# The last two column chunks of a split float32 sequence product as one Strassen step: sums of one operand's tiles made in DRAM, those of the other by VectorE

## The chip, the cores and the metric

One NeuronCore of a Trainium2 chip runs the whole kernel. TensorE multiplies, VectorE, ScalarE and GpSimd (POOL) work on tiles in SBUF, and transfers are issued by SyncE (the SP queue), by ScalarE's queue and, after the change, by POOL's. The metric is the device time of one launch in microseconds (us); a profiled execution gives the span from the first to the last instruction beside it.

## What is computed

```python
a = einsum("bsd,ed->bse", x, dft_hid_re);  b = einsum("bsd,ed->bse", x, dft_hid_im)
y = einsum("ts,bse->bte", dft_seq_re, a) - einsum("ts,bse->bte", dft_seq_im, b)
# peer(x): q = x w_q; scores of 32 heads x 2 halves against 16 keys each; the best 2 of each half,
# the best 2 of the 4 sums, softmax g; act = gelu(x . u[expert]); out = sum g * act * v[expert]
g = sigmoid((x * gate_w).sum(-1))
return g * y + (1 - g) * peer(x)
```

x is 2048 x 640 and both sequence matrices are 2048 x 2048, all float32. Each row of x picks experts out of 256.

## The kernel before

Every large product is made from float32 operands cut in two: `split` lets ScalarE copy the high part (L122) and POOL or VectorE subtract it for the low part (L123). `mm3` then issues three matmuls per tile product, high x high, high x low, low x high (L127 to L129). The sequence product is made first: with C the cosine or sine matrix, C x is computed transposed, in 128 steps n, one per 128 x 512 piece of C. A piece is (w, c, s): w is cosine or sine, c one of four chunks of 512 columns, s one of 16 row tiles. A step has 5 column tiles of x and so 15 matmuls, adding up in 5 PSUM banks over 16 steps; then 5 results of 128 x 512 are copied to the stage tile ST, multiplied by the gate (L192) and stored to DRAM as pd, by w and c. The 16 row tiles of x stay in SBUF in split form (X0 to X15).

The emission order is written by hand. `at(n, f)` puts f behind step n, and engines execute what they are given in order. A piece is loaded five steps ahead by SP (`wf`, L159) and split three steps ahead on POOL into a ring of four (`WS`). Steps 0 to 30 carry the preparation of the query weights beside them; steps 31 (N0) to 63 the scores (15 more matmuls a step), with their selection on VectorE and, every fourth block, the gates (L456 to L486); N1 is 64. From step 64 on the matrices of the hidden product are loaded and split (`load_dd`, `split_dd`, `draw`, `DD`).

Behind that runs `experts`, a background generator that a credit pump (`bg`) advances between groups of matmuls: 32 tiles, each with three VectorE operations that build one-hot tables (`build`, L580 to L582, tile `hot`, four sets), 16 small matmuls on TensorE (`use`, L603) and two VectorE operations that gather the result (`sums`, L589 and L591). Tiles go in pairs: while a pair is being built, the pair before is used. Near the end of the sequence product a `drain` forces out what is left of a tile so that a buffer can change its use.

The hidden product follows as one Strassen–Winograd step (seven half-size products, `UNITS`) for each half of the rows, 70 steps of 9 or 6 matmuls, pieces split five steps ahead into a ring of six. Its sums on the DFT side come from `make_sums` (five VectorE operations, L688 to L692) and `split_sums`, at steps NPC-14 to NPC-5; those on the pd side from `load_parts`, `sum_parts` (L770 to L774) and `store_parts`, at steps 96 to 111, into DRAM tiles pq. NPC is 128 here.

Of the kernel before, what the change touches and what calls it, by code (L numbers as in the profile page):

```python
# [16 lines left out]
P = 128  # L17
# [11 lines left out]
NPC = 2 * NC * NT  # L29
# [6 lines left out]
PAIR = 2 * TC  # L36
NSTEP = 7 * KD
# [53 lines left out]
def gated_mix_kernel(ctx: ExitStack, tc: tile.TileContext, xT, xn, dreT, dimT, wsre, wsim, wq, kT, uT, vv, gw, out):  # L91
# [40 lines left out]
    pq = {u: dram.tile([KD, P, TC], F32, name=f"pq{u}", tag=f"pq{u}") for u in ("s1", "s2", "s4", "s3")}  # L132
# [15 lines left out]
    gt = const.tile([P, NT], F32)  # L148

# [31 lines left out]
    grow, staged, P22 = {}, {}, {}  # L181
# [14 lines left out]
    def store_piece(q):  # L196
        w, c = divmod(q, NC)
        if q == NC + 1:
            P22.update((d, staged[q, d]) for d in range(KD))
        for d in range(KD):  # L200
            nc.scalar.dma_start(pd[w, c][d], staged.pop((q, d)))
# [21 lines left out]
    for q in range(2 * NC):  # L223
# [341 lines left out]
    def experts():  # L565
# [18 lines left out]
        def sums(g, c, t):  # L584
            if c == 0:
                store_gates(g - 1)
                cd[g] = p3.tile([P, E, P], F32, name="cd", tag="cd")
            tmp = p3.tile([P, 8 * E, 4], F32, name="tmp")
            nc.vector.tensor_tensor(tmp, t.rearrange("p m (e t) -> p (m e) t", t=4),  # L589
                                    mask4[:, None, :].to_broadcast([P, 8 * E, 4]), op=OP.mult)  # L590
            nc.vector.tensor_reduce(cd[g][:, :, 8 * c:8 * c + 8].rearrange("p e m -> p m e"),  # L591
                                    tmp.rearrange("p (m e) t -> p m e t", e=E), op=OP.add, axis=AX.X)
            if c == 15:
                summed[g] = cd[g]

        def use(group):
            ts = []
            for g, c, s in group:
                t = bank(7, (P, 8, E * 4)) if last_part else ps_s((P, 8, E * 4))
                pt, qt = (HOT[s // 2][:, s % 2, n].rearrange("p (m c) -> p m c", m=16) for n in range(2))  # L600
                for m in range(16):
                    r = slice(64 * (m % 2), 64 * (m % 2) + 64)
                    nc.tensor.matmul(t[r, m // 2, :], pt[:, m], qt[:, m], start=True, stop=True)  # L603
                ts.append(t)
                free_sets.append(s)
            for (g, c, s), t in zip(group, ts):
                sums(g, c, t)
                yield 1.4
# [24 lines left out]
    def load_dd(m):  # L633

        if m < KD:
            draw[m] = big.tile([P, 2, D], F32, name="draw", tag=("xf", "xh", "xl")[m % 3])
# [13 lines left out]
    for m in range(3):  # L650
        at(N1 + m, load_dd, m)
    for m in range(KD):
        for a in range(2):
            at(N1 + 3 + 2 * m + a, split_dd, m, a)
        at(N1 + 4 + 2 * m, load_dd, m + 3)
# [13 lines left out]
    def load_dt(k):  # L669
        T[k] = big.tile([P, 2, D], F32, name="dt", tag=("xf", "xh")[k % 2])  # L670
        for w in range(2):
            nc.sync.dma_start(T[k][:, w], (dreT, dimT)[w][k])
# [9 lines left out]
    def make_sums(k):  # L682
        if k == 0:
            T["t"] = big.tile([P, 9 * P], F32, name="tf", tag="xl")
        f, t = T.pop(k), T["t"]
# [7 lines left out]
        bg.credit -= 3.0  # L693

    def split_sums(k):
        for n in [k] + ([5 + k // 2] if k % 2 == 0 else []):
            TS[n] = big.tile([P, 2 * D], F32R, name="ts", tag=f"X{(1, 3, 4, 5, 6, 0, 2, 7)[n]}")
# [6 lines left out]
    def load_v():  # L704
        T["f"] = big.tile([P, 2, D], F32, name="dt", tag="xf")
        nc.sync.dma_start(T["f"], vv.rearrange("k p d -> p k d"))

    def split_v():

        for t in ("xh", "xl"):  # L710
            T[t] = big.tile([P, 2, D], F32R, name="v" + t, tag=t)
        split(T["f"], T["xh"], T["xl"], nc.vector)
# [6 lines left out]
    for k in range(KD):  # L719
        at(NPC - 17 + 2 * k, load_dt, k)  # L720
        at(NPC - 14 + 2 * k, make_sums, k)
        at(NPC - 13 + 2 * k, split_sums, k)
    at(NPC - 3, load_v)
    at(NPC, split_v)
    at(NPC + 28, store_gates, 1)


    raw_free, raw_tags = deque(), [("wf", 1)] * 5 + [(f"X{s}", 2) for s in range(10, 16)] + [("xf", 2)]
    raw, sp = {}, {}

    def take(key):
        if raw_tags:
            t, n = raw_tags.pop(0)
            if t == "wf":
                raw_free.append(big.tile([P, TC], F32, name="ra", tag=t, bufs=5))
            else:
                r = big.tile([P, 2, TC], F32, name="ra", tag=t)
                raw_free.extend(r[:, a] for a in range(2))
# [6 lines left out]
    def load_a(b, what, k, row, col):  # L745
        f = take((b, what, k))
        nc.sync.dma_start(f, pd[col - 1, 2 * b + row - 1][k] if row else pq[what][k])
# [7 lines left out]

    PS, parts = [], {}

    def load_parts(k):

        if not PS:  # L760
            PS.extend(big.tile([P, 2, TC], F32, name="ps", tag=t) for t in ("xf", "xh", "xl"))
        parts[k] = [t[:, k % 2] for t in PS]
        for f, q in zip(parts[k], ((0, 1), (0, 0), (1, 0))):
            nc.sync.dma_start(f, pd[q][k])

    def sum_parts(k, n):
        f21, f11, f12 = parts[k]
        f22 = P22[k]
        if n == 0:
            nc.vector.tensor_add(f22, f22, f21)  # L770
            nc.vector.tensor_add(f21, f21, f11)
        else:
            nc.vector.tensor_add(f11, f11, f22)
            nc.vector.tensor_add(f12, f12, f11)  # L774
        bg.credit -= 1.5

    def store_parts(k, n):
        f21, f11, f12 = parts[k]
        for u, f in (("s2", f11), ("s4", f12)) if n else (("s1", P22[k]), ("s3", f21)):
            nc.sync.dma_start(pq[u][k], f)  # L780

    for k, (n, m) in enumerate(((-1, 2), (0, 4), (5, 7), (7, 9), (10, 12))):
        n, m = NT * (NC + 2) + n, NT * (NC + 2) + m
        at(n, load_parts, k)
        for a in range(2):
            at(m + a, sum_parts, k, a)
            at(m + 2 + a, store_parts, k, a)

# [3 lines left out]
    def split_step(m):  # L792
        if m < 2 * NSTEP:
            b, (u, k) = m // NSTEP, divmod(m % NSTEP, KD)
            what = UNITS[u]
            key = (b, "s" if b and what in ("s1", "s2", "s4") else what, k)
            sp[m] = ring(m)[:, 0], ring(m)[:, 1]
            split(raw[key], *sp[m], nc.vector if what in ("s2", "s3") else nc.gpsimd)
            bg.credit -= 0.8 if what in ("s2", "s3") else 0.0
            if b == 0 or what in ("a11", "a12", "a22", "s3", "s4"):  # L800
                give(key)
# [17 lines left out]
    def split_z(b, n):  # L819

        if not zop:
            for k in range(2):
                zop[k] = big.tile([P, 2, TC], F32R, name="zo", tag=f"X{8 + k}")
# [68 lines left out]
    def step(m):  # L892
# [13 lines left out]
        split_step(m + AHEAD)  # L906
# [8 lines left out]
        h, l = sp.pop(m)  # L915
# [23 lines left out]
        if what == "s3":  # L939
            at(NPC + m, post, b, what)  # L940
            at(NPC + m, quarter, b)
        elif not very_last:
            at(NPC + m + 1, post, b, what)
# [11 lines left out]
    def quarter(b):  # L955
        roles["Y"] = [bank(3), bank(4)]
        z_group("Y", 2, None, first=True, last=True)
        at(NPC + b * NSTEP + 6 * KD, post, b, "q")

    M = NPC  # L960
    for k in range(KD):
        at(M - 6 + k, load_a, 0, "a11", k, 1, 1)
        at(M - 4 + min(k, 3), load_a, 0, "a12", k, 1, 2)
        at(M + k // 2, load_a, 0, "s1", k, 0, 0)
        at(M + 2 + k, load_a, 0, "s2", k, 0, 0)
        at(M + 7 + k, load_a, 0, "s4", k, 0, 0)
        at(M + 12 + k, load_a, 0, "s3", k, 0, 0)
        at(M + 18 + k, load_a, 0, "a22", k, 2, 2)
    M = NPC + NSTEP
# [12 lines left out]
    for b in range(2):  # L982
        M = NPC + b * NSTEP
        for n, i in ((0, -1), (1, 21)):
# [25 lines left out]
    last_part = True  # L1010
    for m in range(2 * NSTEP):
        share = 0.95 if m >= 5 else 0.0
        step(m)
        follow(NPC + m)
# [46 lines left out]
```

## Time and profile before

| | |
|---|---|
| device time, 3 runs | 788.47 to 789.88 us, median 788.64 |
| device time of the profiled execution | 788.32 us |
| its span | 786.4 us |
| TensorE busy | 774.7 us (99%), 4116 matmul instructions, mean granted clock 0.996 |
| VectorE, ScalarE, POOL busy | 547.8 us (70%), 275.5 us (35%), 335.9 us (43%) |
| DMA | 130.31 MB, 166 GB/s over the span |

The span is 1.92 us shorter than the device time of the same execution. A busy TensorE counts overlapping matmuls, so the mean duration of one is longer than the distance between two starts; the distance is what a matmul costs. The score steps end near 394 us, the last gates near 421 us, step 85 starts at 465.7 us, and the hidden product starts near 624 us.

### The profile page before, as it was taken

To read this page: it belongs to the slowest core of one execution; us is meant where nothing else is said; L and a number is where in the kernel's file an instruction comes from. 1 tells how busy PE (TensorE), PEld (TensorE's weight loads), DVE (VectorE), ACT (ScalarE), POOL (GpSimd) and SP (SyncE) were. 2 spreads that over 40 slices of the span, in tenths; PEclk is the share of its full clock that TensorE was granted. 3 is DMA by queue.
4 is the path that set the end of the run, shared out by engine and by line. 5 is a ranking of instruction groups with operands and counts; after the bars stand their busy time and mean duration, and the time that the engine had idled before them with its cause. 6 is when DMAs were issued, how large, how long until landed. Compare 5 with 4: busy or idle time off the path is not lost.

```text
span 786.4 us, 11008 instructions
## 1 busy us (share of the span) xinstructions
PE 774.7 (99%) x4116; PEld 624.5 (79%) x4116; DVE 547.8 (70%) x660; ACT 275.5 (35%) x445; POOL 335.9 (43%) x233
## 2 busy tenths in 40 slices
PE   9999999999999999999999999999999899999997
PEld 6777677887888888878888888888888688888886
DVE  6741122287898899999894178799799948836651
ACT  5334323321224524523533711311324353334350
POOL 5423224314414323244159643344456483468270
PEclk9999999999999999999999999999999899999999
DMA  9966995402213142130355342568744695459321
GB/s 347 373 243 189 324 337 187 165 13 88 64 38 99 49 154 83 51 124 29 97 188 171 119 146 85 158 227 277 255 172 162 212 322 185 132 174 320 121 81 67
DMA packets 75508, 130.31 MB, mean 166 GB/s; under 512 B 17088, under 2 KB 24128, under 8 KB 75200
## 3 DMA queue, kind: packets, MB, share of 16 engines
q1 hardware_dynamic: 62704, 112.18, 42.6%
q10 hardware_dynamic: 12752, 17.45, 6.1%
q8 instruction: 32, 0.52, 0.3%
q14 instruction: 20, 0.16, 0.1%
HBM read 102.84 MB, written 25.17 MB: 163 GB/s over the span
## 4 chain that ended last, share of the span: by engine, by line
PE 88%; issue 8%; POOL 2%; DVE 1%; ACT 0%; DMA 0%; ACTq 0%; SPq 0%; DVEq 0%; POOLq 0%
PE b L127 28%; PE b L129 28%; PE b L128 27%; PE b L320 2%; POOL xl L123 2%; PE b L603 1%; PE b L332 1%; PE b L213 0%; DMA wf<-in_wsre 0%; DVE tf L690 0%; DVE tmp L589 0%; ACT L390 0%; ACT WS L122 0%; DVE tf L691 0%; DVE tf L692 0%
## 5 line engine op out<-in xcount | busy, mean ns | idle before, releaser
L123 POOL TENSOR_TENSOR WS<-wf,WS 128x512 fp32r<-128x512 f32 x127 | 190.8, 1508 | 284.8 <-ACT WS L122 284.7
L127 PE MATMUL b<-WS,X 128*128 128x512 f32 x635 | 252.3, 397 | 0.1
L128 PE MATMUL b<-WS,X 128*128 128x512 f32 x635 | 248.6, 391 | 0.0
L129 PE MATMUL b<-WS,X 128*128 128x512 f32 x635 | 248.5, 391 | 0.0
L127 PEld LDWEIGHTS b<-WS,X 128*128 128x128 f32 x635 | 119.9, 189 | 33.1 <-issue 7.8
L129 PEld LDWEIGHTS b<-WS,X 128*128 128x128 f32 x635 | 119.7, 189 | 25.4
L128 PEld LDWEIGHTS b<-WS,X 128*128 128x128 f32 x635 | 120.0, 189 | 23.8 <-POOL WS L123 0.3
L122 ACT ACTIVATE WS<-wf 128x512 fp32r<-128x512 f32 x128 | 79.8, 627 | 145.8 <-PE b L129 66.2
L129 PE MATMUL b<-WU,xl 128*128 128x512 f32 x160 | 63.2, 395 | 2.2 <-POOL xl L123 1.7
L123 POOL TENSOR_TENSOR xl<-xf,xh 128x640 fp32r<-128x640 f32 x16 | 32.1, 2031 | 71.0 <-ACT xh L122 71.0
L127 PE MATMUL b<-WU,xh 128*128 128x512 f32 x160 | 62.4, 390 | 0.0
L128 PE MATMUL b<-WU,xh 128*128 128x512 f32 x160 | 62.3, 390 | 0.0
L423 ACT ACTIVATE sc<-b 128x512 f32<-128x512 f32 x32 | 20.1, 629 | 112.5 <-PE b L129 112.5
L123 POOL TENSOR_TENSOR WS<-ra,WS 128x512 fp32r<-128x512 f32 x32 | 46.0, 1459 | 29.9 <-ACT WS L122 29.2
L437 DVE TENSOR_REDUCE mm<-sc 128x64 f32<-128x1024 f32 x32 | 38.9, 1216 | 26.5 <-ACT sc L423 26.0
L192 DVE SCALAR_TENSOR_TENSOR ST<-ST,grow 128x512 f32<-128x512 f32 x40 | 34.6, 930 | 31.8 <-DMA grow<-gdr 31.8
L335 DVE TENSOR_TENSOR WU<-b,WU 128x512 fp32r<-128x512 f32 (+1 forms) x16 | 7.9, 491 | 56.6 <-ACT WU L334 56.6
L439 DVE TENSOR_TENSOR eq<-sc,mm 128x1024 f16<-128x1024 f32 x32 | 43.4, 1355 | 1.1
L123 POOL TENSOR_TENSOR WP<-ra,WP 128x512 fp32r<-128x512 f32 x18 | 27.7, 1550 | 32.9 <-ACT WP L122 32.7
L443 DVE TENSOR_REDUCE rr<-eq 128x64 f16<-128x1024 f16 x32 | 39.0, 1220 | 1.1
L589 DVE TENSOR_TENSOR tmp<-b,mask 128x512 f32<-128x512 f32 x32 | 22.0, 688 | 25.4 <-PE b L603 24.5
L129 PEld LDWEIGHTS b<-WU,xl 128*128 128x128 f32 x160 | 30.1, 188 | 11.2 <-POOL xl L123 5.1
(148 smaller groups left out, 1244.7 us busy)
## 6 DMA issues: line engine op xcount, KB each, us to landing
wq<-in_wq SPq DMA_DIRECT2D x32, 640.0 KB, 6.7
wf<-in_wsre SPq DMA_DIRECT2D x64, 256.0 KB, 5.2
wf<-in_wsim SPq DMA_DIRECT2D x64, 256.0 KB, 3.6
ra<-pd SPq DMA_DIRECT2D x50, 256.0 KB, 3.4
pd<-ST ACTq DMA_DIRECT2D x40, 256.0 KB, 3.6
xr<-in_xn SPq DMA_DIRECT2D x16, 320.0 KB, 5.8
xf<-in_xT SPq DMA_DIRECT2D x16, 320.0 KB, 3.3
ra<-pqs SPq DMA_DIRECT2D x20, 256.0 KB, 4.3
```

The lines of the kernel that those rows point to most:

```text
L122: nc.scalar.activation(h, f, AF.Copy)
L123: eng.tensor_sub(l, f, h.bitcast(F32))
L127: nc.tensor.matmul(o, wh, ah, start=first, stop=False, skip_group_check=more)
L128: nc.tensor.matmul(o, wh, al, start=False, stop=False, skip_group_check=more)
L129: nc.tensor.matmul(o, wl, ah, start=False, stop=last, skip_group_check=more)
L192: nc.vector.scalar_tensor_tensor(f, f, -1.0 if w else 1.0, g, op0=OP.mult, op1=OP.mult)
L320: nc.tensor.matmul(ps[32 * j:32 * j + 32, :HALF], kp[:, 8 * G // H, r, :], w[:, j], start=(r == 0), stop=(r == 1))
L423: nc.scalar.activation(scs[i].rearrange("p h e -> p (h e)")[:, c], ps, AF.Copy)
L437: nc.vector.tensor_reduce(m, sc, op=OP.max, axis=AX.X)
L439: nc.vector.tensor_tensor(eq, sc, m[:, :, None].to_broadcast([P, HH, E]), op=OP.is_equal)
L443: nc.vector.tensor_reduce(r, eq, op=OP.max, axis=AX.X)
L589: nc.vector.tensor_tensor(tmp, t.rearrange("p m (e t) -> p (m e) t", t=4), mask4[:, None, :].to_broadcast([P, 8 * E, 4]), op=OP.mult)
```

## The change

NPC is now 96: six of the eight chunks are made as before. The last two (sine, columns 1024 to 2047) become one Strassen–Winograd step over a 2 x 2 grid of blocks of C (each 8 row tiles by 512 columns) and of x, in 56 steps G (QS) of 9 matmuls (a11, a12, s1, a22) or 6 (s2, s4, s3): 432 matmuls in place of 480. The hidden product starts at step LP = 152.

- Sums of C's tiles (`cq`, 4 x 8 tiles of 128 x 512) and of pd's (`pq`, 4 x 5 tiles) are made in DRAM: `copy_to` on SP copies a tile, `add_to` on POOL adds another by an accumulating transfer. Most stand in the score steps, five at steps 84 to 88, fifteen in steps G4 to G32. `load_parts`, `sum_parts` and `store_parts` go, with their 20 VectorE operations.
- Sums of x: eight times `load_xs`, `make_xs` (the five operations of `sums_of`, now L719 to L723), `store_xs` into `xq`, at steps 69 to 78; `load_late` and `split_late` bring them back, 40 small pieces split on VectorE at G4 to G35.
- `load_dd` moves from step 64 on to step 77 on, `split_dd` to steps 80 to 91.
- In `experts` each result is gathered by four operations of 128 elements (L596, L598); the last block's rows come earlier, and with them the first build.
- `make_sums` stands every fourth step now, at LP-7+4k. Results of the two chunks are put together in ST (`seq_post`) and stored by `seq_out`.

```diff
-NPC = 2 * NC * NT
+NPC = (2 * NC - 2) * NT
+HT = NT // 2
+QS = 7 * HT
+LP = NPC + QS
...
-            bg.space(lambda a=a: step(a), 5.0 if a else 16.0 if b == NT // NB - 1 else 8.0)
+            bg.space(lambda a=a: step(a), 3.4 if b == NT // NB - 1 else 5.0 if a else 8.0)
...
-            nc.vector.tensor_tensor(tmp, t.rearrange("p m (e t) -> p (m e) t", t=4),
-                                    mask4[:, None, :].to_broadcast([P, 8 * E, 4]), op=OP.mult)
+            nc.vector.tensor_scalar(o, t[:, :, :, 0], mask4[:, 0:1], None, op0=OP.mult)
+            for k in range(1, 4):
+                nc.vector.scalar_tensor_tensor(o, t[:, :, :, k], mask4[:, k:k + 1], o, op0=OP.mult, op1=OP.add)
...
+    for m, n in enumerate((13, 14, 15, 18, 20)):
+        at(N1 + n, load_dd, m)
...
+    def copy_to(t, f):
+        nc.sync.dma_start(t, f)
+    def add_to(t, f):
+        nc.gpsimd.dma_start(t, f, accum_op=OP.add, max_dma_last_dim=2048)
...
+        for i, u in enumerate(("s1", "s2", "s4")):
+            at(NPC + 4 + 2 * (KD * i + k), add_to, q[u], a22)
...
-        at(NPC - 14 + 2 * k, make_sums, k)
+        at(LP - 7 + 4 * k, make_sums, k)
...
+    def load_xs(j):
+        xt[j] = big.tile([P, 2, D], F32, name="xs", tag=("xf", "xh")[j % 2])
+        for a in range(2):
+            nc.sync.dma_start(xt[j][:, a], xn[j + HT * a])
+    def make_xs(j):
+        xt["t"] = t = big.tile([P, 9 * P], F32, name="xt", tag="xl")
+        sums_of(xt.pop(j), t)
+    def store_xs(j):
+        nc.sync.dma_start(xq[j], xt["t"])
...
+    for j in range(HT):
+        n = N1 + 5 + j
+        at(n, load_xs, j)
+        at(n + 1, make_xs, j)
+        at(n + 2, store_xs, j)
...
+    for m in range(QS):
+        share = 0.95
+        seq_step(m)
+        follow(NPC + m)
```

The instruction order shows three places. First VectorE behind the last block of gates. Before, the gating of a chunk (`grow`) and the first builds follow at once:

```order
L482 TENSOR_TENSOR cc<-cc 128x128
L485 CAST gs<-cc 128x4x64
L486 TENSOR_TENSOR gs<-cc,gs 128x4x64
L192 SCALAR_TENSOR_TENSOR ST<-ST,grow 128x512 x5
L580 TENSOR_TENSOR hot_3554<-rows_1202,wtab_152 128x1024
L581 TENSOR_TENSOR hot_3554<-rows_1202,wtab_152 128x1024
L582 TENSOR_TENSOR hot_3554<-hot_3554,rows_1202 128x1024
```

After, five of the eight sums of x stand ahead of the first build; the fifth of them, that build and the start of the sixth (`xs` is the loaded x, `xt` the sums):

```order
L719 TENSOR_TENSOR xt<-xs 128x512
L720 SCALAR_TENSOR_TENSOR xt<-xt,xs 128x256
L721 TENSOR_TENSOR xt<-xt 128x256
L722 TENSOR_TENSOR xt<-xs 128x256
L723 TENSOR_TENSOR xt<-xs 128x128
L586 TENSOR_TENSOR hot_3584<-rows_1258,wtab_208 128x1024
L587 TENSOR_TENSOR hot_3584<-rows_1258,wtab_208 128x1024
L588 TENSOR_TENSOR hot_3584<-hot_3584,rows_1258 128x1024
L719 TENSOR_TENSOR xt<-xs 128x512
```

Builds for the experts now alternate with sums of x, the last of which stands between the second build and the third.

Second SP from step 64 on, where before the loads of C's pieces, `wf`, alternate with the hidden matrices, `draw`:

```order
L159 DMA wf<-in_wsim 128x512 x2
L639 DMA draw<-in_dreT 128x640 x2
L159 DMA wf<-in_wsim 128x512
L639 DMA draw<-in_dreT 128x640 x2
L159 DMA wf<-in_wsim 128x512
```

After, from step 77 on, the stores of the sums of x, `xq`, and the later loads of the hidden matrices stand between them:

```order
L645 DMA draw<-in_dreT 128x640 x2
L991 DMA xq_135<-xt 128x1152
L167 DMA wf<-in_wsim 128x512
L193 DMA grow<-gdr 128x512
L645 DMA draw<-in_dreT 128x640 x2
L991 DMA xq_136<-xt 128x1152
L167 DMA wf<-in_wsim 128x512
L645 DMA draw<-in_dreT 128x640
L645 DMA draw<-in_dimT 128x640
L167 DMA wf<-in_wsim 128x512 x3
```

The last `wf` rows are the pieces of steps 84 to 86; they stand behind a `draw` that takes the buffer of `xt`.

Third POOL, which before has only subtractions from step 96 to the end of the sequence product (those of L123 on `ts` belong to the sums of the hidden matrices):

```order
L123 TENSOR_TENSOR DD<-draw,DD 128x640
L123 TENSOR_TENSOR WS<-wf,WS 128x512 x39
L123 TENSOR_TENSOR ts<-tf,ts 128x256 x2
L123 TENSOR_TENSOR WS<-wf,WS 128x512 x2
L123 TENSOR_TENSOR ts<-tf,ts 128x256 x2
```

After, in the Strassen steps:

```order
L126 TENSOR_TENSOR WS<-ra,WS 128x512 x2
L667 DMA pqs_77<-pd_74 128x512
L126 TENSOR_TENSOR WS<-ra,WS 128x512 x2
L667 DMA pqs_78<-pd_74 128x512
L126 TENSOR_TENSOR WP<-ra,WP 128x512 x2
L667 DMA pqs_79<-pd_74 128x512
```

An accumulating transfer is issued behind every two subtractions there.

More of the change, by code (lines that the diff above doesn't have):

```diff
@@ L221, in seq_piece @@
             run_bg(0.68)
-    for q in range(2 * NC):
+    for q in range(2 * NC - 2):
         n = NT * (q + 1)
@@ L746, in load_a @@
         f = take((b, what, k))
[L747 removed]
+        nc.sync.dma_start(f, pd[col - 1, 2 * b + row - 1][k] if row else pq[what, k])
     def add_a(b, o, what, k, last):
@@ L753, in add_a @@
             give((b, what, k))
[L756 to L775, printed above, removed]
@@ L795, in split_step @@
             what = UNITS[u]
             key = (b, "s" if b and what in ("s1", "s2", "s4") else what, k)
[L797 to L801, printed above, removed]
+            dve = what in ("s2", "s3")
+            last = b == 0 or what in ("a11", "a12", "a22", "s3", "s4")
@@ L803, in gated_mix_kernel @@
+        sp[G] = ring(G)[:, 0], ring(G)[:, 1]
+        split(raw[key], *sp[G], nc.vector if dve else nc.gpsimd)
+        bg.credit -= 0.8 if dve else 0.0
+        if last:
+            give(key)
     zop = {}
@@ new lines, in gated_mix_kernel, with load_c @@
+    for j in range(HT):
+        n = N1 + 5 + j
+        at(n, load_xs, j)
+        at(n + 1, make_xs, j)
+        at(n + 2, store_xs, j)
+        for n in range(4):
+            i = n * HT + j
+            at(NPC + i + 1, load_late, i, n, j)
+            at(NPC + i + 4, split_late, i, n, j)
+    def load_c(what, k):
+        row, col = {"a11": (0, 0), "a12": (0, 1), "a22": (1, 1)}.get(what, (0, 0))
+        f = take(("c", what, k))
+        nc.sync.dma_start(f, wsim[NC - 2 + row, k + HT * col] if what[0] == "a" else cq[what, k])
```

258 lines of the change are left out of this document (189 added, 69 removed).

## Prediction

> **What bounds the kernel now.** I read the page first, its busy shares and the chain that ended last, then what TensorE waited for, then TensorE's own rows in two places.
>
> ```profile
> span 786.4 us, 11008 instructions
> PE 774.7 (99%) x4116; PEld 624.5 (79%) x4116; DVE 547.8 (70%) x660; ACT 275.5 (35%) x445; POOL 335.9 (43%) x233
> ...
> PE 88%; issue 8%; POOL 2%; DVE 1%; ACT 0%; DMA 0%; ACTq 0%; SPq 0%; DVEq 0%; POOLq 0%
> ```
>
> ```profile
> PE b L603 <- DVE tmp L589: 3.7, 2, 2.8
> PE b L129 <- POOL xl L123: 1.7, 3, 0.9
> PE b L277 <- DVE warm L274: 1.2, 1, 1.2
> PE b L213 <- ACT WS L122: 0.5, 1, 0.5
> ```
>
> TensorE is the bound: busy 99%, and all its waits together are 7.1 us of 786.4. So a matmul that goes is a gain at its distance from the next, as long as nothing that it waits for becomes late. That distance stands in the timeline of an undisturbed step, start time first:
>
> ```profile
> 484.59 0.39 PE L128 MATMUL b<-WS,X 128*128 128x512 f32 x1
> ...
> 487.31 0.39 PE L128 MATMUL b<-WS,X 128*128 128x512 f32 x1
> ```
>
> There are 12 intervals between these two starts, 2.72 us, so a matmul costs 0.227 us (the 0.39 us of one overlaps the next). A step of 15 is 3.40 us, of 9 2.04, of 6 1.36.
>
> The longest wait, of 3.7 us, is at the end of the sequence product. By stretch (us; TensorE busy and matmuls; granted clock; DMA):
>
> ```profile
> 612.00:615.00 3.00, 0.77 (x21) 0.67 0.68 190
> 615.00:617.00 2.00, 2.00 (x20) 0.50 0.16 57
> 617.00:619.00 2.00, 2.00 (x6) 0.50 0.04 13
> ```
>
> TensorE idles for over two of three us, and then the clock granted to it is 0.50 for some 4 us. What held it are operations on VectorE, in whose order the experts' L589 stood behind `make_sums`.
>
> **The change, part by part.**
>
> *Matmuls.* 480 become 432: 48 x 0.227 = −10.9 us. The 9- and 6-matmul steps are the form that the hidden product already runs in.
>
> *The old stall.* `make_sums` goes from every second step to every fourth, and the drain to step 92, away from it. The wait is 2.8 + 0.9 us:
>
> ```profile
> 613.35 0.64 PE L603 MATMUL b<-hot 128*64 128x64 f16 x16 [2.82 <-DVE tmp L589]
> 614.87 0.64 PE L603 MATMUL b<-hot 128*64 128x64 f16 x16 [0.88 <-DVE tmp L589]
> 615.44 0.80 PE L127 MATMUL b<-WS,X 128*128 128x512 f32 x1
> ...
> 619.87 0.40 PE L128 MATMUL b<-WS,X 128*128 128x512 f32 x1
> ```
>
> From 615.44 to 619.87 are ten intervals, 4.43 us in place of 2.27: 2.2 us at the low clock, of which I count 2.0. Together −5.7 us; the bound on the other side is 0, if the drain at step 92 waits as long. I take −5.7, since nothing but one build and one gathering stands ahead of it there.
>
> *The sums of x.* This is the part with a price. `make_xs(j+1)` writes the buffer `xt` (one) that `store_xs(j)` reads, so its first operation waits until the transfer has landed; VectorE executes in order, so the builds queue behind it. The same five operations on the same shapes run in `make_sums`:
>
> ```profile
> L688 DVE TENSOR_TENSOR tf<-dt 128x512 f32<-128x512 f32 x5 | 3.4, 683 | 0.0
> L689 DVE SCALAR_TENSOR_TENSOR tf<-tf,dt 128x256 f32<-128x256 f32 x5 | 4.9, 984 | 0.5
> L690 DVE TENSOR_TENSOR tf<-tf 128x256 f32<-128x256 f32 x5 | 4.8, 961 | 0.0
> L691 DVE TENSOR_TENSOR tf<-dt 128x256 f32<-128x256 f32 x5 | 4.8, 958 | 0.0
> L692 DVE TENSOR_TENSOR tf<-dt 128x128 f32<-128x128 f32 x5 | 3.6, 714 | 0.0
> L581 DVE TENSOR_TENSOR hot<-rows,wtab 128x1024 f16<-128x1024 f16 x32 | 35.0, 1093 | 0.0
> L582 DVE TENSOR_TENSOR hot<-hot,rows 128x1024 f16<-128x1024 f16 x32 | 29.5, 921 | 0.0
> L580 DVE TENSOR_TENSOR hot<-rows,wtab 128x1024 f16<-128x1024 f16 x32 | 27.2, 850 | 0.0
> ```
>
> The five means add up to 4.3 us. That is with POOL subtracting on two tracks beside it; where POOL has only a piece per step I take 2.6 us, between 1.9 (estimate: 0.68 for the first, and the four smaller ones by their elements) and 4.3. A build is 1.09 + 0.92 + 0.85 = 2.9 us, 3.2 with one more collision. For the landing of a store of 576 KB the nearest rows are these:
>
> ```profile
> out_y<-ST ACTq DMA_DIRECT2D x7, 512.0 KB, 2.9
> pqs<-ps SPq DMA_DIRECT2D x15, 256.0 KB, 2.5
> ```
>
> By the slope from 256 to 512 KB (0.4 us) a plain store of 576 KB takes 3.05 us. With 0.35 us from VectorE's end to the issue (estimate) one turn of make, issue and landing is 6.0 us, between 5.2 and 7.7 (with landings of 2.9 and 3.05). The emission wants one turn per step of 3.4.
>
> The Trainium skill, page "DMA: Bandwidth & Descriptors", section "Anatomy of one DMA — SWDGE (gpsimd) path", puts a transfer at about 2.0 us and its bytes at 436 GB/s. For 576 KB that gives an estimate of 3.35 us, a turn of 6.3 us and a sum 2.1 us higher than mine; for 512 KB it gives 3.2, where the row above has 2.9, so I stay with the row.
>
> The turns start when the last gates are done:
>
> ```profile
> 341.63 0.28 DVE L456 TENSOR_TENSOR cc<-mm 128x128 f32<-128x128 f32 x1
> ...
> 347.97 0.42 DVE L486 TENSOR_TENSOR gs<-cc,gs 128x256 f16<-128x256 f32 x1
> ...
> 408.22 0.28 DVE L456 TENSOR_TENSOR cc<-mm 128x128 f32<-128x128 f32 x1
> ...
> 421.07 0.42 DVE L486 TENSOR_TENSOR gs<-cc,gs 128x256 f16<-128x256 f32 x1
> ```
>
> The third block of gates took 6.8 us, the last 13.3, beside the subtractions of `DD` on POOL, which now come later. So the last ends near 415 and the first turn starts there. The eighth sum is made at 415 + 2.6 + 7 x 6.0 = 459.6 (453 to 472). In VectorE's order behind it stand, up to the tenth build: 8 builds (25.6 us), a gating of five L192 (4.65 at 930 ns) and three pairs of gatherings (6.3; eight operations a pair at about 0.27 us, estimate from the 0.28 of L456 above). The tenth build is done at 496.2. TensorE needs it in step 90:
>
> ```profile
> 467.79 0.70 PE L603 MATMUL b<-hot 128*64 128x64 f16 x32
> L192 DVE SCALAR_TENSOR_TENSOR ST<-ST,grow 128x512 f32<-128x512 f32 x40 | 34.6, 930 | 31.8 <-DMA grow<-gdr 31.8
> L123 POOL TENSOR_TENSOR WS<-wf,WS 128x512 fp32r<-128x512 f32 x127 | 190.8, 1508 | 284.8 <-ACT WS L122 284.7
> ```
>
> Here the first pair of tiles is used, nine matmuls into step 85, which so begins at 465.7. By the new order pairs are used in steps 82, 84, 87 and 89, 0.69 us each, and the tenth tile's six matmuls into step 90: 465.7 + 5 x 3.40 + 4 x 0.69 + 1.36 = 486.8. The wait is 496.2 − 486.8 = +9.3 us, 0 at a turn of 4.7 us and 21 at 7.7, seven us for each us of a turn.
>
> SP waits in order too: a `draw` takes the buffer of `xt` and so waits for the eighth store, till about 463, and the piece of step 84 is queued behind it: two issues, a landing (2.5 us for 256 KB above), a copy and the subtraction (1.51 in the row above) make it ready near 468, some six us after step 84 could begin. That delay is part of the same 9.3 us, since it moves step 90 as well.
>
> *The accumulating transfers.* Before, no transfer was issued by POOL, so their price on POOL's time is unknown. From G4 to G32 POOL has 22 subtractions, 33.2 us, and TensorE's steps take 53 us; with five steps ahead (some 8.5 us), 15 transfers may hold POOL for 1.9 us each before TensorE waits. The nearest rows are POOL's subtraction (1.51 us) and the landing of `pqs` (2.5 us): from 0 to 15 x 2.5 − 28 = 9.5 us. I take 0, since the queue need not wait for a landing that nothing behind it reads.
>
> The Trainium skill, page "SBUF — State Buffer", section "SBUF: two separate sides", speaks against this part. It says that VectorE and GpSimd share a port under an exclusive lock, and that a transfer issued by GpSimd gets no descriptors while VectorE holds it. No run here shows a transfer from POOL; that operations of the two engines hold each other up the trace agrees with, as far as L581, L582 and L580, three operations on the same shape, spread from 850 to 1093 ns in the mean.
>
> *The rest.* `split_late` (40 small subtractions), the splits on VectorE and the results in ST lie on VectorE, which is 70% busy; `load_parts` and 20 additions go. The experts' gathering changes by little. New small waits: VectorE late at a use, the splits of `draw` beside the builds (POOL then has two subtractions of about 1.5 us in a step of 3.4), the low clock after each wait (2.0 us at the old stall): +2 us, 0 to +7.
>
> **Sum.** 786.4 − 10.9 − 5.7 + 9.3 + 2 = 781.1 us of span. The profiled execution took 788.32, 1.92 more than its span and 0.32 less than the median of the runs: 783.0 us.
>
> **The rivals.**
>
> *The sums of x are hidden.* For it: the lower bounds give 5.2 us a turn, and fewer operations may be in the way of the tenth build than I count. Against: nothing waits only at a turn of 4.7 us, below what the rows give. It gives 781.1 − 9.3 + 1.92 = 773.7 us.
>
> *The turns are longer (slower than before).* The price is 7 us for each us of a turn; the gains less the rest are 10.9 + 5.7 − 2 = 14.6 us, so from 6.0 + (14.6 − 9.3)/7 = 6.8 us on nothing is gained. For it: the means of L689 to L691 are near 1 us, and stores land later beside loads. At 7.5 us the wait is 19.8 and the time 793.5 us. Against: POOL is busy only 43%.
>
> *Accumulating transfers hold POOL.* At 2.5 us each TensorE waits 9.5 us more in G4 to G32: 792.5 us with the 9.3 beside it, 783 without. For it are the collisions that L581 shows; against, the five steps of pieces ahead.
>
> **How the numbers follow.** The forecast 0.50, hidden sums 0.20, longer turns 0.18, held POOL 0.12. A change of 0.2% is 1.6 us, about what a measurement of this kernel tells from none. The forecast's own range is 776 to 789 (turns of 5.2 to 6.5, rest of 0 to 4); of its 0.50, 0.43 is faster, 0.06 the same, 0.01 slower. The hidden sums are faster throughout, longer turns 0.03 the same and 0.15 slower, held POOL 0.05 faster, 0.03 the same and 0.04 slower. Together faster 0.68, same 0.12, slower 0.20. The range from 772 to 796 takes in the hidden sums at their best and turns of 7.7.
>
> **What would show it.** Right: 48 matmuls fewer, at 0.227 us; no wait at the last `make_sums`; L719 on VectorE waiting for `xq` from 415 to 460 at 6 us a turn; TensorE's waits on `hot` or `WS` in steps 83 to 90, some 9 us. Wrong: L719 without idle time ahead of it, or TensorE's waits on `WS` between G4 and G32, behind L667.

## The result, and the profile after

The changed kernel takes 854.34 us (median; 852.98 to 855.01) against 788.56 us: a ratio of 1.083 [1.081, 1.085], 66 us slower. The forecast was 783 us in a range of 772 to 796.

The page of the changed kernel's profile: span, busy times, and the queue that POOL's transfers use, which the kernel before did not have.

```profile
span 853.2 us, 11473 instructions
PE 788.1 (92%) x4068; PEld 624.0 (73%) x4068; DVE 629.7 (74%) x804; ACT 298.2 (35%) x509; POOL 389.3 (46%) x302
...
q0 software_dynamic: 8208, 14.95, 10.7%
```

The 48 matmuls are gone (4116 to 4068), but TensorE is busy for 92% of the span instead of 99%. What it waited for (total us, times, longest):

```profile
PE b L609 <- DVE cd L598: 17.3, 6, 10.1
PE b L130 <- ACT ST L226: 12.6, 1, 12.6
PE b L131 <- POOL WS L126: 6.2, 6, 1.9
PE b L130 <- ACT WS L125: 4.3, 3, 2.7
PE b L130 <- ACT ST L1060: 4.0, 1, 4.0
PE b L131 <- DVE WP L126: 3.7, 1, 3.7
```

The place of the loss shows when both spans are cut at the same events: 147.5 us, where they still agree within half a us, ScalarE's last `act` of the scores, its first copy of the results of steps 79 and 95, and the first matmul of the hidden product (at 628.4 us before; "near 624", ahead of the prediction, was too early). Before (stretch; its length, TensorE busy and matmuls; granted clock; DMA share and GB/s):

```profile
147.50:393.75 246.25, 244.08 (x1181) 1.00 0.24 76
393.75:445.46 51.71, 51.71 (x229) 1.00 0.48 156
445.46:503.27 57.81, 57.81 (x369) 1.00 0.45 145
503.27:628.42 125.15, 121.45 (x764) 0.97 0.62 208
628.42:786.40 157.98, 153.97 (x773) 1.00 0.52 175
```

After, the same five:

```profile
147.50:403.82 256.32, 248.05 (x1183) 0.99 0.56 153
403.82:476.67 72.85, 56.90 (x240) 0.91 0.73 220
476.67:556.05 79.38, 62.76 (x421) 0.89 0.58 173
556.05:683.34 127.29, 115.08 (x636) 0.95 0.78 228
683.34:853.23 169.89, 159.36 (x789) 0.98 0.56 184
```

The scores lose 10.1 us, steps 64 to 79 21.1, steps 80 to 95 21.6, steps 96 to 151 2.1 (although 10.9 us of matmuls are missing there), the hidden product 11.9. (At the first of these cuts TensorE is eleven matmuls further after the change, 240 against 229, so some 2.5 us of the 21.1 belong to the next stage.) Each stage loses in TensorE's busy share, and the three in the middle also in the granted clock (0.89 to 0.95): right behind the longest wait, from 477.3 to 480.4 us, it was 0.50.

In steps 64 to 79, VectorE's sums of x wait as forecast:

```profile
430.82 0.69 DVE L719 TENSOR_TENSOR xt<-xs 128x512 f32<-128x512 f32 x1
443.57 0.69 DVE L719 TENSOR_TENSOR xt<-xs 128x512 f32<-128x512 f32 x1 [10.73 <-DMA xq<-xt]
450.34 0.69 DVE L719 TENSOR_TENSOR xt<-xs 128x512 f32<-128x512 f32 x1 [4.74 <-DMA xq<-xt]
...
481.78 0.69 DVE L719 TENSOR_TENSOR xt<-xs 128x512 f32<-128x512 f32 x1 [3.09 <-DMA xq<-xt]
```

From the first sum to the eighth are seven turns in 51.0 us, 7.3 us each (forecast 6.0): the first takes 12.75 us, the other six 38.2, 6.4 each. SP's own timeline, of the second turn and a bit more, shows why the early ones are long: while transposes are left, the queue has no time of its own:

```profile
442.13 2.40 SPq L504 DMA_TRANSPOSE rt<-rp  x2
444.58 1.22 SPq L504 DMA_TRANSPOSE rt<-gs  x1
445.90 0.52 SPq L991 DMA_DIRECT2D xq<-xt  x1
446.47 1.35 SPq L984 DMA_DIRECT2D xs<-in_xn  x2
447.93 0.50 SPq L167 DMA_DIRECT2D wf<-in_wsim  x1
448.53 2.37 SPq L504 DMA_TRANSPOSE rt<-rp  x2
```

Three transposes cost 3.6 us of issue, the store, the loads of x and the piece of C another 2.4: some 6 us of SP for a step of 3.4. From 456 us on no transposes are left, and SP waits for the sum that it is to store; there the loop through the one buffer sets the pace, 5.4 us in the fifth and the sixth turn. The piece `wf` is last in each turn, so pieces come at the pace of the turns. ScalarE splits them in order, and its copies of the results of step 79 stand behind the copy of a late piece:

```profile
476.13 0.63 ACT L125 ACTIVATE WS<-wf 128x512 fp32r<-128x512 f32 x1 [4.77 <-DMA wf<-in_wsim]
476.67 2.53 ACT L226 ACTIVATE ST<-b 128x512 f32<-128x512 f32 x5
```

TensorE needs those banks and idles for 12.6 us.

In steps 80 to 95 one VectorE operation, a build of a one-hot table, is held for 15 us:

```profile
507.28 1.78 DVE L587 TENSOR_TENSOR hot<-rows,wtab 128x1024 f16<-128x1024 f16 x1
508.98 15.09 DVE L588 TENSOR_TENSOR hot<-hot,rows 128x1024 f16<-128x1024 f16 x1
```

POOL's timeline of the same time, a part of it:

```profile
509.02 1.56 POOL L126 TENSOR_TENSOR WS<-wf,WS 128x512 fp32r<-128x512 f32 x1
510.26 1.84 POOL L126 TENSOR_TENSOR DD<-draw,DD 128x640 fp32r<-128x640 f32 x1
511.77 1.11 POOL L667 DMA_DIRECT2D pqs<-pd  x1
512.33 1.87 POOL L126 TENSOR_TENSOR WS<-wf,WS 128x512 fp32r<-128x512 f32 x1
513.59 2.14 POOL L126 TENSOR_TENSOR DD<-draw,DD 128x640 fp32r<-128x640 f32 x1
515.11 1.38 POOL L667 DMA_DIRECT2D pqs<-pd  x1
```

POOL goes from a piece to a hidden matrix to an accumulating transfer without a gap, and VectorE gets no turn until it is through. TensorE's longest wait of the stage is the end of this, in step 89, where it needs a bank that VectorE empties behind the held build. In the Strassen steps, too, with POOL's transfers beside it, an operation of VectorE is held, a subtraction for a late piece of x:

```profile
528.77 0.64 PE L609 MATMUL b<-hot 128*64 128x64 f16 x16 [10.10 <-DVE cd L598]
577.68 6.42 DVE L126 TENSOR_TENSOR X<-lt,X 128x256 fp32r<-128x256 f32 x1
```

### The profile page after: what moved, and what is told of

The parts are those of the page before. It is cut to its first block, busy times and chain, and to the rows that moved or that the text cites. A ratio compares the mean times of both kernels' runs of the same rounds, so it can differ in the third digit from the quotient of the medians.

```text
span 853.2 us, 11473 instructions
## 1 busy us (share of the span) xinstructions
PE 788.1 (92%) x4068; PEld 624.0 (73%) x4068; DVE 629.7 (74%) x804; ACT 298.2 (35%) x509; POOL 389.3 (46%) x302
## 5 line engine op out<-in xcount | busy, mean ns | idle before, releaser
L126 POOL TENSOR_TENSOR WS<-wf,WS 128x512 fp32r<-128x512 f32 x95 | 143.5, 1513 | 251.7 <-ACT WS L125 245.3
L130 PE MATMUL b<-WS,X 128*128 128x512 f32 x567 | 228.7, 403 | 16.1 <-ACT ST L226 12.6
L131 PE MATMUL b<-WS,X 128*128 128x512 f32 x567 | 225.2, 397 | 6.5 <-POOL WS L126 5.1
L132 PE MATMUL b<-WS,X 128*128 128x512 f32 x567 | 223.9, 395 | 0.0
L130 PEld LDWEIGHTS b<-WS,X 128*128 128x128 f32 x567 | 108.3, 191 | 48.5 <-ACT ST L226 13.6
L131 PEld LDWEIGHTS b<-WS,X 128*128 128x128 f32 x567 | 108.5, 191 | 31.2 <-POOL WS L126 8.2
L126 POOL TENSOR_TENSOR WS<-ra,WS 128x512 fp32r<-128x512 f32 x63 | 94.6, 1522 | 72.5 <-ACT WS L125 68.8
L132 PEld LDWEIGHTS b<-WS,X 128*128 128x128 f32 x567 | 108.4, 191 | 23.2
L125 ACT ACTIVATE WS<-wf 128x512 fp32r<-128x512 f32 x96 | 61.0, 638 | 99.3 <-DMA wf<-in_wsim 40.1
L125 ACT ACTIVATE WS<-ra 128x512 fp32r<-128x512 f32 x84 | 51.0, 626 | 65.9 <-PE b L132 16.1
L429 ACT ACTIVATE sc<-b 128x512 f32<-128x512 f32 x32 | 21.1, 660 | 103.1 <-PE b L132 103.1
L126 POOL TENSOR_TENSOR WP<-ra,WP 128x512 fp32r<-128x512 f32 x31 | 45.9, 1507 | 19.5 <-ACT WP L125 19.5
L588 DVE TENSOR_TENSOR hot<-hot,rows 128x1024 f16<-128x1024 f16 x32 | 50.4, 1575 | 0.0
L509 ACT ACTIVATE rows<-rt 128x384 f16<-128x384 f16 x16 | 31.0, 1940 | 50.3 <-DMA rt<-gs 47.4
L598 DVE SCALAR_TENSOR_TENSOR cd<-b,mask,cd 128x128 f32<-128x128 f32 x96 | 44.7, 466 | 3.4
```

What stands on the lines that cost most here:

```text
L125: nc.scalar.activation(h, f, AF.Copy)
L126: eng.tensor_sub(l, f, h.bitcast(F32))
L130: nc.tensor.matmul(o, wh, ah, start=first, stop=False, skip_group_check=more)
L131: nc.tensor.matmul(o, wh, al, start=False, stop=False, skip_group_check=more)
L132: nc.tensor.matmul(o, wl, ah, start=False, stop=last, skip_group_check=more)
L429: nc.scalar.activation(scs[i].rearrange("p h e -> p (h e)")[:, c], ps, AF.Copy)
```

## The experiments

All are edits of the changed kernel but e13, an edit of the kernel before. The stages are cut as above; where an expectation speaks of the hidden product it counts to the last matmul, some four us less than here (165.8 in the changed kernel).

| run | time us | scores | 64–79 | 80–95 | 96–151 | hidden |
|---|---|---|---|---|---|---|
| before | 788.6 | 246.2 | 51.7 | 57.8 | 125.1 | 158.0 |
| after | 854.3 | 256.3 | 72.9 | 79.4 | 127.3 | 169.9 |
| e1 no sums of x | 821.4 | 259.0 | 53.6 | 72.6 | 119.4 | 168.9 |
| e2 no accumulation | 832.2 | 254.6 | 68.4 | 71.4 | 115.3 | 172.3 |
| e3 no sums in DRAM | 827.3 | 247.7 | 67.8 | 74.2 | 115.4 | 171.9 |
| e4 neither | 798.5 | 246.9 | 52.6 | 64.1 | 114.8 | 169.1 |
| e5 eight buffers | 845.9 | 257.4 | 69.1 | 76.8 | 122.7 | 171.7 |
| e6 copies by POOL | 862.1 | 258.5 | 73.1 | 78.5 | 129.0 | 172.2 |
| e7 sums a step later | 858.7 | 257.5 | 72.9 | 79.2 | 127.1 | 174.9 |
| e8 old gathering | 845.0 | 257.4 | 72.7 | 76.1 | 121.5 | 168.2 |
| e9 x by POOL | 846.3 | 257.6 | 60.9 | 81.7 | 125.4 | 172.5 |
| e10 matmuls and splits | 787.0 | 247.9 | 52.6 | 66.2 | 112.0 | 159.6 |
| e11 five adds later | 846.5 | 256.6 | 72.9 | 74.0 | 124.9 | 169.0 |
| e12 repairs together | 836.8 | 259.5 | 58.8 | 78.4 | 123.2 | 169.1 |
| e13 before, early end | 789.7 | 247.4 | 51.7 | 57.8 | 118.8 | 165.4 |
| e14 e10, early end | 781.8 | 246.9 | 52.6 | 60.9 | 109.4 | 162.2 |
| e15 free transfers | 845.0 | 259.2 | 69.9 | 77.8 | 116.9 | 173.6 |

### Leaving out the sums: e1 to e4

```diff
-        at(n, load_xs, j)                                                       # e1, e4
-        at(n + 1, make_xs, j)                                                   # e1, e4
-        at(n + 2, store_xs, j)                                                  # e1, e4
-        nc.gpsimd.dma_start(t, f, accum_op=OP.add, max_dma_last_dim=2048)       # e2, e3, e4
-        nc.sync.dma_start(t, f)                                                 # copy_to: e3, e4
```

> Left out of the changed kernel: the making of the sums of x (load_xs, make_xs, store_xs); the late pieces are loaded from x itself, in the same number and size. Theory S (the turns of the sums of x, through one buffer, hold VectorE, SP and with SP the pieces of C): steps 64 to 79 fall from 72.3 us back to about 51, steps 80 to 95 from 84.5 to about 62, since what was late there came from the backlog; about 810 us in all. Theory P (POOL's subtractions and transfers in steps 84 to 92 hold VectorE by themselves): steps 64 to 79 fall by 21 too, but steps 80 to 95 stay at 75 or more; 825 us or more.

> Left out of the changed kernel: the 57 accumulating transfers; the copies in DRAM stay. If it is the accumulating transfers that delay the score steps (copies on SP wait until an addition has landed), their 256.9 us fall to about 247, and the 15 us in which one VectorE operation was held near 510 us shrink to under 6; about 830 us. If the amount of data is the cause, the score steps stay above 252 us.

> Left out of the changed kernel: all sums in DRAM, copies and accumulating transfers; pieces are loaded from unsummed tiles in the same number and size. Score steps 247 us under every theory that puts their loss on these transfers. Theory S: steps 64 to 79 still take about 70 us, and steps 80 to 95 at least 75; about 830 us. If the DRAM sums were the main cause of the whole loss, it would come out under 795 us.

> Left out of the changed kernel: the sums of x as in e1_no_xsums and the sums in DRAM as in e3_no_dram_sums; the matmuls, the late pieces and the order of the rest stay. If these two carry the loss, what is left is the gain of 48 matmuls and the old stall less the waits of the Strassen steps: 775 to 788 us. If it stays above 800 us, the loss lies in the Strassen steps and the hidden product (late pieces and subtractions on VectorE).

e1 gives steps 64 to 79 back (53.6) but leaves steps 80 to 95 at 72.6, nearer to Theory P (75 or more) than to Theory S (62): an operation is held for 10.8 us, and TensorE then waits 8.5. In e2 and e3 no single operation of VectorE takes over 3 us, so the hold needs the accumulating transfers. In e3, which has the sums of x but no hold, TensorE waits 5.7 us for VectorE's gathering in steps 80 to 95, against 3.5 in e4, which has neither. e3 heals the scores (247.7), e2 hardly (254.6). e4 is still ten us slower than before: its hidden product, 169.1 us, keeps nearly the whole loss. Leaving out the sums of x alone saves 32.9 us, those in DRAM alone 27.0, both 55.8 of the 66; without them the change still does not pay.

### Buffer or queue: e5 and e9

```diff
-        xt["t"] = t = big.tile([P, 9 * P], F32, name="xt", tag="xl")
+            xt["t"] = big.tile([P, HT, 9 * P], F32, name="xt", tag="WU")        # once; sum j uses [:, j]
-            nc.sync.dma_start(xt[j][:, a], xn[j + HT * a])
+            nc.gpsimd.dma_start(xt[j][:, a], xn[j + HT * a])                    # e9 only, store_xs too
-        at(n + 2, store_xs, j)
+        at(n + 3, store_xs, j)                                                  # e9 only
```

> The changed kernel with eight buffers for the sums of x (in the space of the query weights, which the scores no longer need) in place of one; nothing left out. If the one buffer makes the turns (a sum waits for the landing of the store before), the idle time of VectorE before L719 goes, steps 64 to 79 fall from 72.9 us to about 54, and the whole to about 825 us, near the kernel without the sums (821). If the turn is made by the loads of x on SP, steps 64 to 79 stay above 66 us and the whole above 843.

> The changed kernel with eight buffers for the sums of x, and with the loads of x and the stores of its sums issued by POOL in place of SP (the stores a step later). Nothing left out. If SP's order makes the turns (transposes of 1.2 us each to issue, loads of x, a store that waits for VectorE, and behind them the piece of C), steps 64 to 79 fall from 69.1 us in e5_xt_eight_buffers to 56 or less, and the whole to about 833. If VectorE or the transfers themselves make the turn, they stay above 65. POOL may lose time at the issues, seen as waits on the low parts of WS.

The buffer was worth 3.7 us of the stage's 21, not 19. With eight buffers VectorE waits for the loads of x instead, which SP issues late. Taking x off SP gives 8.2 us more: four pieces of C are then issued in one go at 451 us, although the eighth sum starts no sooner (at 474.1 us, in e5 at 472.9). But steps 80 to 95 take 81.7, and the whole is no faster than e5. The last 9 us of the stage stay: SP still issues the transposes, and ScalarE's copies of their results hold its copies of pieces up.

### The hold of VectorE: e11

```diff
-        at(NT * (NC + 1) + 4 + k, add_to, q["s4"], a12)
+        at(NT * (NC + 1) + 12 + k, add_to, q["s4"], a12)
```

> The changed kernel with the five accumulating transfers of steps 84 to 88 moved to steps 92 to 96, behind the subtractions of the hidden matrices. Nothing left out. If the hold of 15 us of one VectorE operation needs POOL to run without a gap (subtractions of pieces and hidden matrices and, between them, issues of transfers), no operation is held over 8 us in steps 80 to 95, which fall from 79.4 to about 72 us, and the whole to about 847. If POOL's subtractions hold it by themselves, the hold of 15 us and the time stay.

With the five transfers moved away from the subtractions of the hidden matrices, no operation in the same place takes over 2.1 us; in time order three of the builds there:

```profile
509.94 2.06 DVE L588 TENSOR_TENSOR hot<-hot,rows 128x1024 f16<-128x1024 f16 x1
511.92 1.77 DVE L586 TENSOR_TENSOR hot<-rows,wtab 128x1024 f16<-128x1024 f16 x1
513.62 2.06 DVE L587 TENSOR_TENSOR hot<-rows,wtab 128x1024 f16<-128x1024 f16 x1
```

The stage falls by 5.3 us, the whole by 7.9. The hold is gone although POOL's subtractions follow each other without a gap here too:

```profile
509.42 2.02 POOL L126 TENSOR_TENSOR DD<-draw,DD 128x640 fp32r<-128x640 f32 x1
511.41 1.74 POOL L126 TENSOR_TENSOR WS<-wf,WS 128x512 fp32r<-128x512 f32 x1
513.11 2.02 POOL L126 TENSOR_TENSOR DD<-draw,DD 128x640 fp32r<-128x640 f32 x1
```

So subtractions alone cost VectorE's operations one of them each (1.8 to 2.1 us in place of 0.68), and it takes both kinds of POOL work together to shut VectorE out. How a transfer among them takes VectorE's turn away is not shown. In the Strassen steps, where the transfers stay, a late piece is still held for 6.4 us in e11.

### The transfers of the score steps: e6 and e15

```diff
-        nc.sync.dma_start(t, f)
+        nc.gpsimd.dma_start(t, f)                                       # e6: copy_to
+        nc.sync.dma_start(scratch(), wsim[0, len(fr) % NT])             # e15: copy_to; add_to the same by POOL
```

> The changed kernel with the copies in DRAM issued by POOL in place of SP; nothing left out, the same transfers. If the score steps lose their 10 us because the copies wait on SP ahead of the transposes, and ScalarE's copies of scores stand behind those, they fall from 256.3 to 250 us or less. If the transfers themselves slow the transposes down, they stay at 254 or more. POOL's waits may show as waits of TensorE on the low parts.

> The changed kernel with each of the copies and accumulating transfers in DRAM replaced by a plain copy of an input tile to a scratch tile of its own: the same number, size, issuing queue and place, but nothing waits for another and nothing is summed (pieces are loaded from unsummed tiles). If the score steps lose 10 us because the transfers wait for each other on SP and POOL, they fall from 256.3 to 249 or less. If the traffic itself slows the transposes and the other loads, they stay at 253 or more; the 15 us hold of VectorE then stays too, since POOL still issues among its subtractions.

Neither helps: 258.5 and 259.2 us. So it is not that one sum waits for another. (In e15, where POOL issues plain transfers, the hold is shared by two operations of 5.4 and 4.5 us.) The landing of SP's transposes in the score steps (150 to 395 us; count, median us), before and after (the last line is from what ScalarE waited for):

```profile
rt<-rp SPq DMA_TRANSPOSE x24, 2.4
rt<-gs SPq DMA_TRANSPOSE x12, 2.3
```

```profile
rt<-rp SPq DMA_TRANSPOSE x24, 4.8
rt<-gs SPq DMA_TRANSPOSE x12, 4.1
...
ACT rows L509 <- DMA rt<-gs: 28.8, 6, 13.9
```

In e15 they land in 4.0 and 2.4 us. ScalarE waits for them (28.8 us in all, 16.1 before), and behind these waits stand its copies of scores and of the high parts `xh`. TensorE's waits in the score steps grow from 1.7 to 8.0 us: 2.1 for the copies of scores, 2.8 for `xh`, 3.1 for POOL's low parts, which follow them. e2, which has copies on SP and no accumulation, lands the transposes in 2.8 and 2.4, yet ScalarE waits as long for them (28.9) and 8 us are lost; e6, with SP free of copies, in 5.4 and 5.2. How much of the 10 us is landing and how much SP's time stays open; that they go with the transfers altogether (e3) is shown.

### VectorE's load: e8 and e10

```diff
-            nc.vector.tensor_scalar(o, t[:, :, :, 0], mask4[:, 0:1], None, op0=OP.mult)
-            for k in range(1, 4):
-                nc.vector.scalar_tensor_tensor(o, t[:, :, :, k], mask4[:, k:k + 1], o, op0=OP.mult, op1=OP.add)
+            tmp = p3.tile([P, 8 * E, 4], F32, name="tmp")               # and the two operations of before
...
-            at(NPC + i + 1, load_late, i, n, j)                         # e10 only, with the edits of e4
-            at(NPC + i + 4, split_late, i, n, j)
```

> The changed kernel with the experts' results gathered as before, by two VectorE operations of 512 elements (0.69 us each) in place of four of 128 (0.44 to 0.49 each). Nothing left out. VectorE then saves some 0.5 us for each of 32 tiles, 16 us. If VectorE is the bound of steps 80 to 151, TensorE's waits behind the gathering (19 us in all) fall by half or more and the whole to about 842 us; if those waits come from single held operations, the time stays within 4 us of 854.

> Left out of the changed kernel: sums of x, sums in DRAM (as in e4_neither) and the late pieces of x (no loads, no small subtractions; the tiles of x are used as they are); the experts' results are gathered as before. What is left of the change are its matmuls, its splits of C and the putting together of results. If VectorE's added work is what ate the gain in e4_neither (798 us), steps 80 to 95 fall to 60 us, steps 96 to 151 from 114.8 to 107 or less, the whole to 780 to 786 us. If the Strassen steps wait for other reasons (the order on ScalarE, the banks), it stays above 790.

The groups of the gathering, after (busy us, mean ns), and then before:

```profile
L598 DVE SCALAR_TENSOR_TENSOR cd<-b,mask,cd 128x128 f32<-128x128 f32 x96 | 44.7, 466 | 3.4
...
L596 DVE TENSOR_SCALAR cd<-b,mask 128x128 f32<-128x128 f32 x32 | 14.1, 440 | 6.6 <-PE b L609 4.5 <-PE b L132 2.1
```

```profile
L589 DVE TENSOR_TENSOR tmp<-b,mask 128x512 f32<-128x512 f32 x32 | 22.0, 688 | 25.4 <-PE b L603 24.5
L591 DVE TENSOR_REDUCE cd<-tmp 128x128 f32<-128x512 f32 x32 | 22.0, 688 | 5.0 <-DMA gd<-cd 3.9
```

For the 32 tiles four operations of 128 elements take 58.8 us, two of 512 take 44.0. e8 gives back 9 us, between its two expectations. e10 gives 11.5 against e4, 9.5 of it in the hidden product, where it seems VectorE's backlog was paid; it leaves out two things at once, and no run parts them. But at 787.0 us, ratio 0.996 [0.994, 0.998], the bare skeleton of the change is only just faster than before, between the two expectations.

### The stall at the drain: e7, e13 and e14

```diff
-        at(LP - 7 + 4 * k, make_sums, k)
+        at(LP - 6 + 4 * k, make_sums, k)                                # e7, split_sums too
-        ending = n >= NPC - 8
+        ending = n >= NPC - 16                                          # e13 on before, e14 on e10
```

> The changed kernel with make_sums and split_sums of the hidden matrices one step later, so that ScalarE's copy of the last result bank stands ahead of its copies for split_sums. Nothing left out. If that order makes TensorE's wait of 4.0 us (7.1 in e4_neither) at the start of the hidden product, it goes to under 0.5 us and the hidden product falls from 165.8 by 4 to 7 us; about 849 us in all. If the wait is for VectorE in any order, it only moves.

> The kernel before, with the experts put into their one-tile-at-a-time mode 16 steps before the end of the sequence product in place of 8, so that the two sets that the drain must free are free long before. Nothing left out. If the stall of 3.7 us and the low clock behind it come from tiles that the drain forces out behind make_sums, both shrink and the time falls by 2 to 5 us, to 784 to 787. If VectorE is late there in any order, the wait only moves and the time stays within 1 us of 788.6.

> e10_matmuls_and_splits with the same early mode; left out is the same as there (sums of x, sums in DRAM, late pieces; the gathering as before). If the drain at step 92 is what the old stall became, TensorE's waits of 485 to 498 us (4.4 us and a low clock) shrink and the time falls from 787 to 780 to 783, so that most of the 10.9 us of the matmuls shows. If VectorE's work in steps 80 to 95 is the bound in any order, it stays at 785 or more.

e7 moves the wait at the start of the hidden product and makes others (3.4, then 3.1 us); 858.7 us. TensorE's rows of e10 in step 91:

```profile
495.26 0.44 PE L609 MATMUL b<-hot 128*64 128x64 f16 x16 [1.29 <-DVE tmp L595]
497.15 0.64 PE L609 MATMUL b<-hot 128*64 128x64 f16 x16 [1.44 <-DVE tmp L595]
```

Here the one-tile mode, which begins at step 88, has a pair used early, so that the drain behind step 92 finds its sets free. With the mode begun eight steps sooner these waits go: e14 takes 781.8 us, 0.990 [0.989, 0.992], 5.2 less than e10. The same edit on the kernel before takes away its stall of 3.7 us (steps 96 to 127 fall from 125.1 to 118.8), and the hidden product gives it all back (161.4 against 154.0, both to the last matmul): 789.7 us, 1.0004 [0.999, 1.0015].

### The repairs together: e12

e9, e8's gathering and e11's transfers in one kernel.

> The changed kernel with the repairs together: x loaded and stored by POOL with eight buffers, the gathering as before, the five accumulating transfers later. Nothing left out. If the effects add up (21 less 4 us, 9 us, 7 us), about 818 us; the score steps (10 us over before) and VectorE's load in the Strassen steps stay, so it is still slower than before. If what was late at one place only becomes late at the next, over 830.

836.8 us: 17.5 less than the change, where the expectation added up 36 and the three repairs alone gave 25 (8.0, 9.3 and 7.9). What was late at one place became late at the next: steps 80 to 95 take 78.4 us, against 74.0 in e11. No run that computes the whole reference beats the kernel before.

## Why the prediction was wrong

Two steps failed. The sums of x were priced at 9.3 us, as a wait for the tenth build; of the 21.1 us that steps 64 to 79 lost, 19.3 are theirs (e1), by late pieces of C. The sums in DRAM were priced at nothing; with them the scores lose 8.6 us and VectorE is shut out for 15.1. Term by term:

- **Matmuls, −10.9.** They went, but even with all sums, the late pieces and the new gathering left out only 7.7 of the 16.6 us of the first two terms show (e14, against 789.5 for the kernel before beside it).
- **The old stall, −5.7.** Wrong. I moved the drain to step 92 and counted one build and one gathering ahead of it. In the new order VectorE gathers twelve tiles in steps 80 to 95 in place of eight, at 1.8 us each in place of 1.4, and the one-tile mode ahead of the drain finds it late: TensorE waits 1.4 us in step 90 of the changed kernel, 3.1 and 1.1 there in e11, 1.3 and 1.4 in step 91 of e10. And at the last `make_sums`, where I expected no wait, there is one again, the 4.0 us on L1060 above: ScalarE copies a result bank behind splits for which it waits 4.9 us for VectorE. e13 shows that the old stall was not to be had either: without it, the hidden product takes 7.4 us longer.
- **The sums of x, +9.3.** Direction and the loop through the buffer were right; in the two turns where that loop alone counts it took 5.4 us, and over all seven 7.3, inside the range of 5.2 to 7.7. (The 0.35 us up to the issue came from no row; the store's issue takes 0.33 us in these turns, and its landing 3.7 in the median, not 3.05.) Size and path were not right: the stage lost 21.1 us, of which the buffer makes 3.7 (e5), and TensorE's wait of 12.6 us is for the banks of step 79. The term failed at two points. The start was to be 415 us; it was 430.8, since the scores ended 10.1 us late and the gates took 11.4 us, not 6.8, even without the hidden matrices beside them. And I gave SP's queue one late piece, inside the 9.3. Every piece of the turn stands behind a store, and three transposes at 1.2 us each were not in my sum of SP's time at all. That TensorE waits 10.1 us in step 89, so near to the 9.3 foreseen for step 90, is luck: it stands behind the held build, and e1, without sums of x, has a wait of 8.5 us behind such a build. (Two slips in the sum are small: by the instruction order the first pair is used twelve matmuls into step 85, not nine, and 24 gatherings at 0.27 us are 6.5 us, not 6.3; the wait would have come to some 10 us.)
- **The accumulating transfers, 0.** Wrong twice. I asked whether POOL has time for them, and it has. With the copies they cost the score steps 8.6 us (e3), where I did not look, and among POOL's subtractions they took VectorE's turns (15.1 us, gone in e11). Of the rivals the held POOL was nearest: it named the collisions but the wrong victim.
- **The rest, +2.** I wrote that the gathering changes by little, with 0.27 us for an operation; it is 0.44 to 0.47. My row's operands lie side by side in SBUF, while here one is every fourth element of a bank of matmul results. Which difference makes the price no run shows; the bank alone does not, since 512 elements of one take 0.69 us (L589), as 512 from SBUF do (L719). Against the gathering before that is 15 us of VectorE, and 9 us of the time (e8). Without sums, the gathering and the late pieces together make 11.5 us (e4 to e10).
- The Trainium skill, page "SBUF — State Buffer", section "SBUF: two separate sides", says that a transfer issued by GpSimd starves while VectorE holds the shared port. The trace shows the two engines holding each other up, but the other way round: POOL's issues took 0.8 to 2.0 us throughout, and VectorE's operation starved. The section's rule that the first to start keeps the pair for one instruction does not by itself give 15 us.

The common error was to price the parts against the queues of the kernel before, one by one, with VectorE at 70% as cover for the last of them. From 480 to 680 us after the change it is busy 93%; but from 480 to 624 us before it was already 90%, so the cover was not there.

## What to carry to other kernels

When work is taken from the bound engine and paid for on the others, add up each other engine's and each issuing queue's time in the stage where the payment falls, issue time of transposes included, and compare it with the length of that stage, not with the span. In-order queues turn one late store into late loads of everything behind it, so a new store that waits for compute does not belong ahead of the loads that feed the bound engine. A stall that an earlier tile explains is only gone when the late engine has less to do; otherwise it moves.

## What the runs showed of the hardware

- A VectorE operation of 0.68 us was held for 15.1 us by a POOL that ran subtractions and transfer issues without a gap; with the issues left out or moved away, no more than one subtraction held it at that place (1.8 to 2.1 us), though the subtractions had no gap either.
- Issuing one transpose took SP 1.2 us, a plain transfer 0.3 to 0.7.
- The transfers of the sums, 18 MB more in the score steps, doubled the landing of transposes there, from 2.4 to 4.8 us, at a DMA share of only 0.56; without the accumulating ones (e2) it was 2.8.
